# Decay factors of q applied in its turn, a completion signal moved to ScalarE, and one normalisation step issued one product later

## The chip, the cores and the metric

The kernel runs on one core of a Trainium2 chip. The metric is the device time of one execution in microseconds (us), the median of several executions. All runs of this study are recorded as fast (mean granted clock 0.986 to 1.0), so fast runs are compared with fast runs. The engines are TensorE (PE, with its weight loads as PEld), VectorE (DVE), ScalarE (ACT), GpSimd (POOL) and SyncE (SP), which issues most transfers (812 of 846 in the built program of the kernel before).

## The reference

Retention attention over 8 batches, 8 heads, 576 positions and a head size of 64 is followed by a SwiGLU feed-forward layer on the 4608 rows that result (cut to what matters):

```python
def _attn_ref(q, k, v):
    scores = scale * np.matmul(q, k.transpose(0, 1, 3, 2))
    Dmat = np.where(rel >= 0, gamma[:, None, None] ** rel[None, :, :], 0.0)
    return np.matmul(scores * Dmat[None], v)

def _moe_ref(x, w_gate, w_val, w_out, rms_g):
    xn = x / np.sqrt(np.mean(x * x, axis=-1, keepdims=True) + 1e-06) * rms_g
    g = xn @ w_gate
    return (g / (1.0 + np.exp(-g)) * (xn @ w_val)) @ w_out
```

## The kernel before

Attention runs in 32 jobs (a batch and a pair of heads each), in chunks of 64 positions. Jobs 0 to 7 come first, in the first 60 us, while weights are loaded and rounded beside them. The other jobs are strewn between the matmuls of the feed-forward layer, which works in combinations of weight blocks and of x (Strassen-like products, named x, y, z and w).

A job has these bursts of 64x64 matmuls on PE: scores and states, then values (the part within a chunk) and carried (what earlier chunks bring), both into the PSUM tile `av`. Jobs 0 to 7 have a turn ahead, which transposes q and k:

```python
    def turn(j):
        ...
                for e in range(2):
                    nc.tensor.matmul(
                        ps[side(e), c::NFULL], lhsT=d["q"][:, e, c], rhs=ident,
                        start=True, stop=True,
                    )
            t = d[nm + "T"] = att.tile([P, S], F32, tag=nm + "T", name=f"{nm}T_{j}")
            nc.scalar.copy(out=t[:, : NFULL * P], in_=ps)
        ...

    def values(j):
        ...
        d["valued"] = nc.gpsimd.memset(tick, 0.0)      # waits for the last matmul of values
        follow(d["valued"], mm)                        # carried's first matmul waits for it

    def carried(j):
        ...                                            # matmuls into av, then x on VectorE:
                    nc.vector.tensor_tensor(
                        out=x[to, first - c0 // L :: 2],
                        in0=av[odd][at, i * L : (i + n) * L].rearrange("p (c k) -> p c k", k=L),
                        in1=g.to_broadcast([at.stop - at.start, n, L]), op=ALU.mult,
                    )
```

In the stage from 217 to 260 us the last product group of the first row block, job 8, the weight combining on GpSimd (`combine`) and the scaling of the next block's x (`norm_2`) meet:

```python
        combine(1)
        slot(8, rest=False)
        following(8)
        for i, _ in enumerate(rest):
            if i == 2:
                norm_2(2)
        combine(0)
        slot(9)
```

Of the kernel before, what the change touches and what calls it, by code (L numbers as in the profile page):

```python
# [10 lines left out]
F32 = mybir.dt.float32  # L11
U32 = mybir.dt.uint32
AF = mybir.ActivationFunctionType
ALU = mybir.AluOpType
P = 128
L = P // 2


def _gamma(H):
    return 1.0 - 2.0 ** (-5.0 - np.arange(H, dtype=np.float64))  # L20


def _decay_tables(H, D):



    pairs = _gamma(H).reshape(H // 2, 2).T
    rows = np.repeat(pairs, D, axis=0)
    pos = np.arange(L)
    p = np.concatenate([pos, pos])  # L30
    gq = rows[:, :, None] ** (pos + L) / np.sqrt(D)
    t = pairs.T[None] ** -p[:, None, None], rows**L, gq, np.roll(gq, D, axis=0)
    return [np.ascontiguousarray(x).astype(np.float32) for x in t]


def _causal_table():

    return np.ascontiguousarray(np.tile(np.triu(np.ones((L, L), np.float32)), (2, 1)))
# [3 lines left out]
def kernel(  # L42
# [11 lines left out]
    nc = tc.nc  # L54
    B, H, S, D = q.shape
    NTOK, DM = out.shape
    DFF = moe_w_gate.shape[1]
    NHP = H // 2
    NF = DFF // P
    NC = S // L  # L60
    NFULL = S // P
    TAIL = S - NFULL * P
# [12 lines left out]
    const = ctx.enter_context(tc.tile_pool(name="const", bufs=1))  # L75
# [23 lines left out]
    ident = const.tile([P, P], F32, name="ident")  # L99
    mean_w = cell("mean_w", 1.0 / DM)  # L100
    mhalf = cell("mhalf", -0.5)
# [3 lines left out]
    causal = const.tile([P, L], F32, name="causal")  # L105
    gq = const.tile([P, NHP, L], F32, name="gq")
    gx = const.tile([P, NHP, L], F32, name="gx")
    gv = const.tile([P, NHP, 2], F32, name="gv")
    gc = const.tile([P, NHP], F32, name="gc")
    tick = const.tile([1, 1], F32, name="tick")  # L110
    rms_g = const.tile([P, NHP], F32, name="rms_g")
    w_out = const.tile([P, NF, DM], F32, name="w_out")
# [12 lines left out]
    w_up = [const.tile([P, 7 * 2, NH * P], F32, name=n) for n in ("w_gate", "w_val")]  # L125

    jobs = [(b, hp) for b in range(B) for hp in range(NHP)]
# [40 lines left out]
    def find_places():  # L168

        n = NFULL * 2 * D  # L170
        kv = {
            nm: [raw.tile([P, n], F32, tag=nm, name=f"first_{nm}_{i}", bufs=bufs) for i in range(bufs)]
            for nm, bufs in (("k", 4), ("v", 3))
        }
        other = raw.tile([P, S], F32, tag="qraw", name="first_k_7")[:, :n]
        sums = [ffn.tile([P, 3 * 2 * HU], F32, tag=t, name=f"first_{t}") for t in ("sums", "t1")]
        room = h_of[0].rearrange("p f t -> p (f t)")[:, 2 * NHP * 4 * P :]
        more = w_up[1][:, 8:].rearrange("p b f -> p (b f)")[:, 6 * DM :]
        return {
            "k": kv["k"] + kv["v"] + [other],  # L180
            "v": [t[:, i * n : i * n + n] for t in sums for i in range(2)]
            + [more[:, i * n : i * n + n] for i in range(3)] + [room],
        }
# [16 lines left out]
    def load_kv(j):  # L200
# [12 lines left out]
            out=t, in_=v[b, 2 * hp : 2 * hp + 2, NFULL * P :].rearrange("e p d -> p e d")  # L213
        )

    def turn(j):

        d = st[j]
        last = bank(f"turn_{j}_t")
        for nm in "qk":  # L220
            ps = bank(f"turn_{j}_{nm}")
            for c in range(NFULL):
                if nm == "k":
                    nc.tensor.transpose(
                        out=ps[:, c * P : c * P + P],
                        in_=d["k"][:, c].rearrange("p e d -> p (e d)"), identity=ident,
                    )
                    continue
                for e in range(2):
                    nc.tensor.matmul(  # L230
                        ps[side(e), c::NFULL], lhsT=d["q"][:, e, c], rhs=ident,
                        start=True, stop=True,
                    )
            t = d[nm + "T"] = att.tile([P, S], F32, tag=nm + "T", name=f"{nm}T_{j}")
            nc.scalar.copy(out=t[:, : NFULL * P], in_=ps)
        for i, nm in enumerate("qk"):
            o = slice(i * TAIL, i * TAIL + TAIL)
            nc.tensor.transpose(
                out=last[:, o], in_=d[nm + "t"].rearrange("p e d -> p (e d)"),
                identity=ident[:TAIL, :TAIL],  # L240
            )
        for i, nm in enumerate("qk"):
            o = slice(i * TAIL, i * TAIL + TAIL)
            nc.scalar.copy(out=d[nm + "T"][:, NFULL * P :], in_=last[:, o])
# [22 lines left out]
    def side(i):  # L267
        return slice(i * L, i * L + L)
# [75 lines left out]
    def values(j):  # L344

        d = st[j]
        av = d["av"] = [bank(f"av_{j}_{i}") for i in range(2)]
        for c in range(NC):
            i, odd = divmod(c, 2)
            for e in range(2):  # L350
                mm = nc.tensor.matmul(  # L351
                    av[odd][column(j, odd, e), i * L : i * L + L],
                    lhsT=d["v"][side(odd), i, e] if c < NC - 1 else d["vt"][:, e],
                    rhs=d["ret"][side(odd), e, i],
                    start=(c < 2), stop=False, skip_group_check=True,
                )


        d["valued"] = nc.gpsimd.memset(tick, 0.0)
        follow(d["valued"], mm)  # L360

    def carried(j):

        d = st[j]
        b, hp = jobs[j]
        av = d["av"]
        for c in range(1, NC):
            i, odd = divmod(c, 2)
            for e in range(2):
                mm = nc.tensor.matmul(  # L370
                    av[odd][column(j, odd, e), i * L : i * L + L], lhsT=d["sum"][side(e), c - 1],
                    rhs=d["qT"][side(e), c * L : c * L + L],
                    start=False, stop=(c >= NC - 2), skip_group_check=True,
                )
                if c == 1 and e == 0:
                    follow(mm, d["valued"])
        for c0, c1 in ((0, 2 * HU), (2 * HU, S)) if b % 2 == 0 else ((0, HU), (HU, S)):
            u, o = divmod(b * S + c0, U)
            if u not in x_of:
                x_of[u] = xp.tile([P, NHP, U], F32, tag="x", name=f"x_{u}")  # L380
            x = x_of[u][:, hp, o : o + c1 - c0].rearrange("p (c k) -> p c k", k=L)
            for first in (c0 // L, c0 // L + 1):
                i, odd = divmod(first, 2)
                n = -(-(c1 // L - first) // 2)
                moves = [(slice(0, P),) * 2]
                if column(j, odd, 0) != side(0):
                    moves = [(side(e), column(j, odd, e)) for e in range(2)]
                for to, at in moves:
                    g = (gq if to == at else gx)[at, hp].unsqueeze(1)
                    nc.vector.tensor_tensor(  # L390
                        out=x[to, first - c0 // L :: 2],
                        in0=av[odd][at, i * L : (i + n) * L].rearrange("p (c k) -> p c k", k=L),
                        in1=g.to_broadcast([at.stop - at.start, n, L]), op=ALU.mult,
                    )
        st[j] = {}
# [307 lines left out]
    for g in range(NG):  # L703
        for m, src in enumerate((moe_w_gate, moe_w_val)):
            for half in range(2):
                n = (half * NH + 2 * g) * P
# [31 lines left out]
    def load_chunks(n, queue=nc.scalar):  # L738

        nonlocal n_loads  # L740
        while n_loads < min(n, len(chunks)) and waits_at.get(spare(n_loads)) is None:
            load_chunk(n_loads, queue)
            n_loads += 1
# [102 lines left out]
    def start():  # L846

        h_of[0] = ffn.tile([P, NF, U], F32, tag="h", name="h_0")
        tables = list(zip((causal, gv, gc, gq, gx), (_causal_table(), *_decay_tables(H, D))))

        def table(i, queue):
            t, values_ = tables[i]
            src = nc.inline_tensor(values_, name=t.tensor.name + "_table")
            queue.dma_start(out=t, in_=src.ap())
# [5 lines left out]
        for _ in range(6):  # L860
            nc.tensor.matmul(warm[:, :P], lhsT=ones, rhs=ones, start=True, stop=True)
        first_places.update(find_places())
        load_chunks(1)
        for i in (1, 0, 2):
            table(i, nc.scalar)
        weights(3)
        for j in range(2 * NHP):
            load_first(j, {0: range(2), 1: range(2, H), NHP: range(H)}.get(j))
            if j == 1:
                table(3, nc.sync)  # L870
            load_chunks((1, 1, 1, 1, 2, 2, 2, 3)[j], nc.sync)
        table(4, nc.sync)
        nc.sync.dma_start(out=rms_g, in_=moe_rms_g.rearrange("(c p) -> p c", p=P))
        load_chunks(4, nc.sync)
# [4 lines left out]
        for j in range(2 * NHP):  # L879
# [7 lines left out]
            if j:  # L887
                u, c = divmod(j - 1, NHP)
# [54 lines left out]
        slot(8, rest=False)  # L943
        following(8)
        for i, _ in enumerate(rest):
            if i == 2:
                norm_2(2)
        combine(0)
        slot(9)
# [72 lines left out]
```

## Time and profile before

| | before |
|---|---|
| median time | 1151.92 us (1151.08 to 1154.7, 3 runs; with the fourth, of the result below, 1152.18) |
| span of the profiled run | 1151.4 us |
| PE busy | 1126.5 us, 98% |
| largest PE waits | issue 5.6 us in the first 60 us, tick 3.15 us, k of job 0 2.4 us |

The prediction below shows the lines for these. One line that it doesn't show turns out to matter, the line of the DMA queue that carries instructions (packets, MB, share of the engines' time):

```profile
q8 instruction: 83, 1.36, 0.5%
```

83 packets of 1.36 MB make 16.4 KB each. PE has 10524 multiplications and as many weight loads in the trace, and 167 waits and branches in the built program, 21,215 instructions in all: 21,215 / 83 = 255.6 instructions a packet. From these two counts I estimate that the queue carries PE's instruction stream in blocks of 256; the times of its packets, further below, agree.

### The profile page before, as it was taken

The page shows a single profiled execution, that of the slowest core. Times are in us where ns is not written, and L with a number is a line of the kernel's source. Part 1 is how long each engine was busy: PE and PEld are TensorE (multiplying, and loading weights), DVE is VectorE, ACT ScalarE, POOL GpSimd, SP SyncE. Part 2 cuts the span into 40 slices and gives each one's busy share as a digit, 9 for nine tenths or more (in the row PEclk, how much of TensorE's full clock was granted, in tenths as well). Part 3 has the DMA queues.
Part 4 walks back from the last instruction along what each step waited for, and adds up shares of the span by engine and source line. Part 5 has one row for each costly group of instructions (what it writes and reads, how often), then busy time and mean ns, then how long its engine had stood idle before and what let it go on. Part 6 is the DMA issues. An engine that isn't in the chain of part 4 may idle for free.

```text
span 1151.4 us, 24802 instructions
## 1 busy us (share of the span) xinstructions
PE 1126.5 (98%) x10524; PEld 1053.4 (91%) x10524; DVE 716.0 (62%) x1420; ACT 244.0 (21%) x480; POOL 50.8 (4%) x74
## 2 busy tenths in 40 slices
PE   8799999989999999999999999999999999999998
PEld 6655557989999999999999999999999999999998
DVE  5788858675675675365766675465576566445352
ACT  5546542002201211211221120120220220120210
POOL 0000000570000000000000000000000000000000
PEclk8999999999999999999999999999999999999999
DMA  8764336335453565044345456306436503403304
GB/s 203 207 184 147 109 131 193 56 59 117 115 130 67 146 141 160 1 105 102 97 119 73 116 144 119 114 29 120 117 80 140 144 19 93 128 1 99 122 1 110
DMA packets 292943, 125.42 MB, mean 109 GB/s; under 512 B 270432, under 2 KB 275808, under 8 KB 292832
## 3 DMA queue, kind: packets, MB, share of 16 engines
q1 hardware_dynamic: 282688, 107.66, 38.1%
q10 hardware_dynamic: 10144, 16.16, 4.3%
q8 instruction: 83, 1.36, 0.5%
q14 instruction: 28, 0.23, 0.1%
HBM read 108.83 MB, written 14.94 MB: 108 GB/s over the span
## 4 chain that ended last, share of the span: by engine, by line
PE 90%; DVE 3%; DMA 2%; POOL 1%; ACT 1%; issue 1%; SPq 0%; DVEq 0%; POOLq 0%; ACTq 0%
PE x L507 14%; PE w L507 14%; PE z L507 13%; PE up L564 8%; PE xo L629 8%; PE wo L629 7%; PE zo L629 7%; PE y L507 7%; PE yo L629 4%; PE av L351 2%; PE av L370 2%; PE s L280 2%; POOL w_gate L811 1%; PE s L300 1%; DMA w_gate<-in_moe_w_out_dram 1%
## 5 line engine op out<-in xcount | busy, mean ns | idle before, releaser
L531 ACT COPY m<-x 128x384 f32<-128x384 f32 x60 | 28.8, 479 | 449.8 <-PE x L507 425.5
L629 PE MATMUL xo<-h,w_out 128*128 128x192 f32 x528 | 90.3, 328 | 0.0
L507 PE MATMUL w<-sums,w_val 128*128 128x192 f32 x480 | 88.6, 328 | 0.6 <-DVE c L514 0.3
L507 PE MATMUL x<-x,w_gate 128*128 128x192 f32 x480 | 89.0, 329 | 0.0
L507 PE MATMUL x<-x,w_val 128*128 128x192 f32 x480 | 88.8, 328 | 0.0
L507 PE MATMUL z<-x,w_gate 128*128 128x192 f32 x480 | 87.8, 326 | 0.0
L507 PE MATMUL w<-sums,w_gate 128*128 128x192 f32 x480 | 87.8, 326 | 0.0
L507 PE MATMUL z<-x,w_val 128*128 128x192 f32 x480 | 87.8, 326 | 0.0
L629 PEld LDWEIGHTS xo<-h,w_out 128*128 128x128 f32 x528 | 85.9, 190 | 0.6
L629 PE MATMUL wo<-h,w_out 128*128 128x192 f32 x504 | 85.3, 326 | 0.0
L629 PEld LDWEIGHTS wo<-h,w_out 128*128 128x128 f32 x504 | 82.5, 190 | 0.0
L514 DVE TENSOR_TENSOR u<-m,y 128x384 f32<-128x384 f32 x60 | 33.1, 552 | 79.2 <-PE y L507 79.1
L507 PEld LDWEIGHTS w<-sums,w_val 128*128 128x128 f32 x480 | 79.2, 190 | 2.9 <-DVE c L514 2.9
L507 PEld LDWEIGHTS x<-x,w_gate 128*128 128x128 f32 x480 | 79.6, 191 | 0.5
L507 PEld LDWEIGHTS z<-x,w_gate 128*128 128x128 f32 x480 | 79.8, 190 | 0.0
L507 PEld LDWEIGHTS x<-x,w_val 128*128 128x128 f32 x480 | 79.1, 190 | 0.6
L507 PEld LDWEIGHTS z<-x,w_val 128*128 128x128 f32 x480 | 79.6, 190 | 0.0
L507 PEld LDWEIGHTS w<-sums,w_gate 128*128 128x128 f32 x480 | 79.6, 190 | 0.0
L514 DVE TENSOR_TENSOR h<-u,w 128x384 f32<-128x384 f32 x60 | 33.0, 551 | 71.0 <-PE w L507 71.0
L526 ACT ACTIVATE h<-h 128x384 f32<-128x384 f32 x90 | 47.1, 523 | 88.6 <-DVE h L514 88.6
L564 PE MATMUL up<-x,w_gate 128*128 128x384 f32 x192 | 63.3, 488 | 0.9 <-DVE x L476 0.7
L564 PE MATMUL up<-x,w_val 128*128 128x384 f32 x192 | 62.7, 487 | 0.2 <-ACT w_val L572 0.2
(170 smaller groups left out, 1769.8 us busy)
## 6 DMA issues: line engine op xcount, KB each, us to landing
w_out<-w_blocks SPq DMA_DIRECT2D x70, 768.0 KB, 5.1
out_dram<-o SPq DMA_DIRECT2D x368, 24.0 KB, 1.6
qraw<-in_q_dram SPq DMA_DIRECT2D x96, 72.0 KB, 2.7
kraw<-in_k_dram SPq DMA_DIRECT2D x96, 72.0 KB, 2.8
k<-in_k_dram SPq DMA_DIRECT2D x48, 128.0 KB, 3.0
v<-in_v_dram SPq DMA_DIRECT2D x48, 128.0 KB, 2.9
w_out<-in_moe_w_gate_dram ACTq DMA_DIRECT2D x5, 1024.0 KB, 5.8
w_out<-in_moe_w_out_dram ACTq DMA_DIRECT2D x3, 1024.0 KB, 4.9
```

Source lines behind the costliest of these rows:

```text
L280: nc.tensor.matmul(s[side(odd), e, i * L : i * L + L], lhsT=d["kT"][side(e), c * L : c * L + L], rhs=d["qT"][side(e), c * L : c * L + L], ...
L300: nc.tensor.matmul(o[side(e)], lhsT=d["k"][side(odd), i, e], rhs=d["v"][side(odd), i, e], start=True, stop=True,)
L351: mm = nc.tensor.matmul(av[odd][column(j, odd, e), i * L : i * L + L], lhsT=d["v"][side(odd), i, e] if c < NC - 1 else d["vt"][:, e], rhs= ...
L370: mm = nc.tensor.matmul(av[odd][column(j, odd, e), i * L : i * L + L], lhsT=d["sum"][side(e), c - 1], rhs=d["qT"][side(e), c * L : c * L + L],
L507: nc.tensor.matmul(ps[:, i * HU : i * HU + HU], lhsT=w_up[m][:, 2 * blk + c, cut], rhs=t_of[u][blk][:, c], start=(start and i == c == 0), ...
L514: nc.vector.tensor_tensor(out=o, in0=a, in1=pairs_of(ps), op=ALU.add)
L526: nc.scalar.activation(out=o, in_=c, func=AF.Silu)
L531: nc.scalar.copy(out=s1, in_=pairs_of(x_))
L564: nc.tensor.matmul(ps[:, :U], lhsT=w_up[m][:, 4 * half + c, i * P : i * P + P], rhs=x_of[u][:, c], start=(c == 0), stop=(c == NHP - 1),)
L629: nc.tensor.matmul(ps[:, i * HU : i * HU + HU], lhsT=a[:, c, i * P : i * P + P], rhs=rhs[:, c], start=(start and i == c == 0), stop=False, ...
L811: nc.gpsimd.tensor_tensor(out=o, in0=a, in1=b, op=op)
```

## The change

Its intent was threefold: to take the multiplication of x by q's decay off VectorE in the eight first jobs, by putting the factors into the matmul that turns q; to free job 8's carried from GpSimd's queue; and to scale x of block 2 one product later, so that zo no longer waits behind it. Core of the diff, with cuts marked:

```diff
+    def make_factors(j):
+        for e in range(2):
+            main, tail = factors(j, e)
+            g = turned[:, 2 * jobs[j][1] + e]
+            if j < 2:
+                for i in range(NFULL):
+                    nc.scalar.activation(
+                        out=main[:, i], in_=ident, func=AF.Copy, scale=g[:, i : i + 1]
+                    )
 ... (one more for the tail; GpSimd tensor_tensor for j >= 2)
-                        ps[side(e), c::NFULL], lhsT=d["q"][:, e, c], rhs=ident,
+                        ps[side(e), c::NFULL], lhsT=d["q"][:, e, c], rhs=factors(j, e)[0][:, c],
 ... (the tail of q: two 64x64 matmuls in place of one transpose)
-        d["valued"] = nc.gpsimd.memset(tick, 0.0)
+        if j == 2 * NHP:
+            d["valued"] = nc.scalar.copy(out=tick, in_=mhalf[:1])
+        else:
+            d["valued"] = nc.gpsimd.memset(tick, 0.0)
 ... (x of jobs 0 to 7: nc.scalar.copy in place of nc.vector.tensor_tensor)
+        for i in (5, 1, 0, 2):
+            table(i, nc.scalar)
         load_chunks(1)
-        for i in (1, 0, 2):
-            table(i, nc.scalar)
+        for j in range(NHP):
+            make_factors(j)
 ...
-            if i == 2:
+            if i == 3:
                 norm_2(2)
```

More of the change, by code (lines that the diff above doesn't have):

```diff
@@ L32, in _decay_tables @@
     t = pairs.T[None] ** -p[:, None, None], rows**L, gq, np.roll(gq, D, axis=0)
+    at = np.stack([(4 * np.arange(P) + i) % L for i in range(4)] + [np.arange(P) % L], axis=1)
+    t += (_gamma(H)[None, :, None] ** (at[:, None, :] + L) / np.sqrt(D),)
     return [np.ascontiguousarray(x).astype(np.float32) for x in t]
@@ L109 @@
     gc = const.tile([P, NHP], F32, name="gc")
+    turned = const.tile([P, H, NFULL + 1], F32, name="turned")
     tick = const.tile([1, 1], F32, name="tick")
@@ L214, in load_kv, with factors @@
         )
+    def factors(j, e):
+        h = 2 * jobs[j][1] + e
+        main = w_up[0][:, h, 2 * P : 6 * P].rearrange("p (i t) -> p i t", t=P)
+        return main, w_up[1][:TAIL, h, 4 * P : 4 * P + TAIL]
+    def make_factors(j):
[7 more added lines that the diff above has]
+                    )
+                nc.scalar.activation(
+                    out=tail, in_=ident[:TAIL, :TAIL], func=AF.Copy, scale=g[:TAIL, NFULL:]
+                )
+                continue
+            nc.gpsimd.tensor_tensor(
+                out=main, in0=ident.unsqueeze(1).to_broadcast([P, NFULL, P]),
+                in1=g[:, :NFULL].unsqueeze(2).to_broadcast([P, NFULL, P]), op=ALU.mult,
+            )
+            nc.gpsimd.tensor_tensor(
+                out=tail, in0=ident[:TAIL, :TAIL],
+                in1=g[:TAIL, NFULL:].to_broadcast([TAIL, TAIL]), op=ALU.mult,
+            )
     def turn(j):
@@ L235, in turn @@
             nc.scalar.copy(out=t[:, : NFULL * P], in_=ps)
-        for i, nm in enumerate("qk"):
-            o = slice(i * TAIL, i * TAIL + TAIL)
-            nc.tensor.transpose(
-                out=last[:, o], in_=d[nm + "t"].rearrange("p e d -> p (e d)"),
-                identity=ident[:TAIL, :TAIL],
-            )
+        for e in range(2):
+            nc.tensor.matmul(
+                last[side(e), :TAIL], lhsT=d["qt"][:, e], rhs=factors(j, e)[1],
+                start=True, stop=True,
+            )
+        nc.tensor.transpose(
+            out=last[:, TAIL : 2 * TAIL], in_=d["kt"].rearrange("p e d -> p (e d)"),
+            identity=ident[:TAIL, :TAIL],
+        )
         for i, nm in enumerate("qk"):
@@ L388, in carried @@
                 for to, at in moves:
+                    if j < 2 * NHP:
+                        nc.scalar.copy(
+                            out=x[to, first - c0 // L :: 2],
+                            in_=av[odd][at, i * L : (i + n) * L].rearrange("p (c k) -> p c k", k=L),
+                        )
+                        continue
                     g = (gq if to == at else gx)[at, hp].unsqueeze(1)
@@ L848, in start @@
         h_of[0] = ffn.tile([P, NF, U], F32, tag="h", name="h_0")
-        tables = list(zip((causal, gv, gc, gq, gx), (_causal_table(), *_decay_tables(H, D))))
+        tables = list(zip((causal, gv, gc, gq, gx, turned), (_causal_table(), *_decay_tables(H, D))))
         def table(i, queue):
@@ L868, in start @@
             load_first(j, {0: range(2), 1: range(2, H), NHP: range(H)}.get(j))
-            if j == 1:
-                table(3, nc.sync)
             load_chunks((1, 1, 1, 1, 2, 2, 2, 3)[j], nc.sync)
+        table(3, nc.sync)
         table(4, nc.sync)
```

## The prediction

> **What bounds the kernel now.** The engine table of the page comes first, because it says which engine can matter at all.
>
> ```profile
> PE 1126.5 (98%) x10524; PEld 1053.4 (91%) x10524; DVE 716.0 (62%) x1420; ACT 244.0 (21%) x480; POOL 50.8 (4%) x74
> ```
>
> TensorE (PE) is busy for 98% of 1151.4 us, so only its 25 us of idle time, its matmul count and its clock can change the end. VectorE (DVE), ScalarE (ACT) and GpSimd (POOL) count only where PE waits for them. Next, the table of PE's waits, summed by releaser (total, count, longest):
>
> ```profile
> PE av L370 <- issue: 4.1, 3, 2.3
> PE av L370 <- POOL tick L359: 3.7, 3, 3.1
> PE turn_k L224 <- DMA first_k<-in_k_dram: 2.4, 1, 2.4
> PE s L280 <- issue: 1.4, 2, 1.0
> ...
> PE av L351 <- ACT kT L235: 1.1, 4, 0.3
> PE zo L629 <- DVE u4o L638: 0.8, 1, 0.8
> PE s L280 <- ACT kT L235: 0.8, 1, 0.8
> ```
>
> The largest removable wait is one of 3.1 us on the tick. It sits in the stage at 217 to 260 us, read from the timeline of all engines (start, duration, line, what, and in brackets the idle time before):
>
> ```profile
> 235.03 17.56 POOL L811 TENSOR_TENSOR w_gate<-w_gate 128x512 f32<-128x512 f32 x12
> ...
> 237.07 1.50 DVE L487 TENSOR_TENSOR sums<-x,sums 128x384 f32<-128x384 f32 x1
> ...
> 241.22 2.28 DVE L641 TENSOR_TENSOR h<-h 128x1152 f32<-128x1152 f32 x1
> ...
> 243.69 4.06 PE L629 MATMUL wo<-h,w_out 128*128 128x192 f32 x24
> ...
> 252.53 0.09 POOL L359 MEMSET tick<- 1x1 f32 x1
> 252.67 0.69 PE L370 MATMUL av<-qT,sum 64*64 64x64 f32 x32 [3.15 <-POOL tick L359]
> ```
>
> The tick is a 0.09 us memset queued behind 17.56 us of GpSimd's weight combining. The stretch-by-stretch view shows what the wait costs afterwards:
>
> ```profile
> 253.00:254.00 1.00, 1.00 (x31) 0.93 (x21) 0.55 (x2) 0.00 (x0) 0.00 (x0) 1.00 0.39 64
> 254.00:255.00 1.00, 1.00 (x6) 1.00 (x5) 0.94 (x4) 0.00 (x0) 0.00 (x0) 0.61 0.30 46
> 255.00:256.00 1.00, 1.00 (x5) 1.00 (x4) 0.88 (x5) 0.48 (x1) 0.00 (x0) 0.50 0.06 5
> ```
>
> The third column from the end is the granted clock. It is 0.50 from about 254.4 to 257.7, and eight matmuls that take 1.30 us elsewhere take 2.0 and then 2.48: some 1.9 us lost. The tick thus costs 3.15 + 1.9 = 5.0 us. The start is the other stage, on ScalarE's timeline:
>
> ```profile
> 7.90 0.33 ACTq L854 DMA_DIRECT2D causal<-causal_table  x1
> 8.28 0.44 ACTq L854 DMA_DIRECT2D gc<-gc_table  x1
> 8.76 0.59 ACT L235 COPY qT<-turn_q 128x512 f32<-128x512 f32 x1 [6.54 <-DMA gv<-gv_table]
> 9.24 0.59 ACT L235 COPY kT<-turn_k 128x512 f32<-128x512 f32 x1
> ```
>
> Job 0's scores start at 9.89, right after these copies. ScalarE is busy without a gap until 17.37; from there PE sets the pace, about 5.9 us a job.
>
> [...] L487 takes 1.50 us under the combining and .557 elsewhere, L641 2.28 against 1.33, while L638, with one input in PSUM, keeps .55. [...] The "issue" waits of PE (0.35, 1.07, 2.33, 1.01 and 0.81 in the first 60 us, 5.6 in all) lie at regular distances in the instruction stream[...].
>
> **The change, part by part.**
>
> *Factors in the turn.* q's decay now comes from the right-hand side of the matmul that turns q, a diagonal of factors instead of the identity. The 16 matmuls a job stay; the tail has one more 64x64 matmul, about .05 us, 8 x .05 = +0.4. The diagonals of the first two head pairs are 16 ACTIVATEs of 128x128 and 4 of 64x64, and they stand in ScalarE's queue before the first qT copy. From rows with a scale operand (128x256 at a pitch of .41, 64x64 at .24) I interpolate .295 for 128x128: 16 x .295 + 4 x .24 = 5.7 us. They follow, in the same queue, the issue of the first weight chunk, which waits for the second half of k_0. That landed at 7.9 in the kernel before, in competition with the chunk; with the chunk held back I estimate 5.0 to 5.5 (393 GB/s moved at 4 to 6 us). So qT is copied at 5.5 + 5.7 = 11.2 instead of 8.76: +2.4. The whole ScalarE-bound start shifts by it. GpSimd's diagonals (pairs 2 and 3) take about 4 x 1.6 us, from 19.29/12 for a 128x512 operation, and are ready by 15, well before job 2.
>
> *x by ScalarE, other buffer waits.* For jobs 0 to 7 four VectorE multiplications (.94 us a job) become four ScalarE copies. VectorE is full only at 50 to 67 us, where values(7) waited 0.55 and the first up products 0.71; I give back 0.3 of these. The order of the instructions moves too: PSUM banks of the turn rotate differently, so that in slots 2 to 7 the turn's tail no longer waits for the qT copy (0.15 a slot) nor the values for the kT copy (0.24): 6 x 0.39 = -2.3. The states will instead sometimes wait for v's scaling on ScalarE, at an estimate of +0.1 a slot, +0.6. Net of this part with the added matmuls: -2.3 + 0.6 + 0.4 - 0.3 = -1.6.
>
> *Tick by ScalarE.* Job 8's tick now follows its values at once: -5.0 with the clock loss, and it is all on PE's path.
>
> *x of the second half scaled one product later.* PE no longer waits 0.8 for u4o. But the scaling and sums now stand on VectorE behind u2o, u4o, c and T, which come at the end of yo, 234.2. Chain: these four 2.3, scaling 4 x .55 = 2.2, sums .61 + 3 x 1.51 = 5.1 (GpSimd combines until 252.5), T .58, h of L641 2.3, together 12.5, so h is ready at 246.7 and wo starts about 246.9 to 247.8, against 243.69. PE runs dry at 242.6: an idle of 4.3 to 5.2 us and[...] a half clock afterwards worth 1.5 to 1.9. From wo on: 4.0, values and scores 1.8, carried .7, x and y 2.6, clock 1.5: y ends at about 258.0, where it ended at 257.84. So the tick's gain is given back: net of these two parts 0 (+-1.5).
>
> Sum: 1151.9 + 2.4 - 1.6 + 0 = 1152.7.
>
> **The rivals.**
> 1. The tick's 5 us come through. [...] It would make 1152.7 - 5 = 1147.7, with the start as estimated.
> 2. The start is not the bound. The loads of q, k and v run until 52 us, and ScalarE waited for v of job 5 at 36 to 38, so a late start may be taken up by later waits: -2.4, or 1150.3. Against it: PE had hardly a DMA wait after 8.02.
> 3. Bad luck in the instruction fetch. 52 more ScalarE instructions, 32 fewer VectorE ones and other loads shift where PE's blocks fall against full DMA queues: the 5.6 us may become 3 or 9, with a clock loss of up to 2 behind any longer one: 1150 to 1157.
> 4. ScalarE's start costs more: the chunk's issue at 6.5 rather than 5.5, and chunk 0's rounding, now later, delays qT_1. +2, or 1154.7.
>
> **Range and chances.** The central value is the sum, drawn 0.4 towards rivals 1 and 2, which both lie lower: 1152.3. Errors are about 2 for the start, 1.5 for the 217 to 260 stage, 2.5 for fetch and clock, 1 for the slots; in quadrature 3.6, and 1.28 x 3.6 = 4.6, so 1147.7 to 1156.9. Two per cent is 23 us, more than all terms together, so "within 2%" is nearly certain.
>
> **What would show it.** Right: the first qT copy at about 11.2 behind 20 ACTIVATEs; no tick wait at carried(8); wo waiting 4 us for DVE's L641 with L487 still near 1.5 us; y of job 8 ending some 1 to 3 us later than 257.84 by the clock of the span only because of the start. Wrong: a wo that follows zo at once (rival 1), a PE that stands at the same time at 62 us as before despite the late start (rival 2), or "issue" waits whose sum differs from 5.6 by more than 3 (rival 3).

## The result

The changed kernel is correct and slower: 1164.17 us median (1161.17 to 1165.04, 4 runs) against 1152.18. The ratio is 1.0096, with a 95% interval of 1.0071 to 1.0121. Ratios here are the mean time of one kernel's fast runs over the mean of the other's fast runs of the same rounds, so not quite the ratio of the medians quoted. That is "within 2%", but it lies well outside the predicted range of 1147.7 to 1156.9.

The engine line of the page:

```profile
PE 1133.6 (98%) x10548; PEld 1060.5 (91%) x10548; DVE 709.1 (61%) x1388; ACT 255.3 (22%) x533; POOL 56.0 (5%) x81
```

VectorE has 32 instructions less and ScalarE 53 more, as planned. PE has 24 more multiplications and 24 more weight loads, 48 instructions, because 16 float32 matmuls, with two records each in the trace, take the place of 8 transposes with one record each. By the built programs there are also 12 more waits (179 against 167). Keep the sum, 60, in mind. PE's waits in the changed kernel (total, count, longest):

```profile
PE av L409 <- issue: 7.3, 4, 3.0
PE wo L674 <- DVE h L686: 4.7, 1, 4.7
PE turn_q L263 <- ACT w_gate L233: 3.1, 2, 2.4
...
PE s L316 <- ACT kT L268: 1.2, 1, 1.2
PE x L552 <- issue: 1.1, 1, 1.1
...
PE z L552 <- DVE u L559: 0.6, 1, 0.6
```

The tick's 3.1 is gone, the wait of wo for h is there, and "issue" in carried (L409) has grown. Where the time came from is read by the start of the same PE instruction in both traces:

| PE instruction | before | after | offset |
|---|---|---|---|
| scores of job 0 | 9.89 | 12.78 | +2.89 |
| mean square of block 0, second half | 67.45 | 69.85 | +2.40 |
| mean square of block 2 | 204.79 | 207.35 | +2.56 |
| z of job 8's slot | 257.68 | 262.05 | +4.37 |
| a mean square | 329.97 | 333.95 | +3.98 |
| another | 600.79 | 604.10 | +3.31 |
| another | 694.73 | 700.69 | +5.96 |
| another | 870.93 | 880.51 | +9.58 |
| another | 963.98 | 974.52 | +10.54 |

So 2.6 us come in the start and 1.8 in the stage around 240 us (2.7 by values of job 9, 273.38 before and 278.62 after). Until 600 us 1.9 are won back, most of them where a stall of the kernel before, in job 10, is gone. Then 7.2 come between 600 and 970 us, where the change has no line at all.

**The late part.** PE's timeline there, one line for each of the four stalls, with what runs ahead of it (start, duration, line, what, count of records, idle time before):

```profile
652.79 0.56 PE L409 MATMUL av<-qT,sum 64*64 64x64 f32 x23
654.73 0.34 PE L409 MATMUL av<-qT,sum 64*64 64x64 f32 x8 [1.37 <-issue]
...
676.97 0.34 PE L409 MATMUL av<-qT,sum 64*64 64x64 f32 x5 [1.24 <-issue]
...
846.11 0.35 PE L409 MATMUL av<-qT,sum 64*64 64x64 f32 x9 [1.71 <-issue]
...
931.99 0.65 PE L552 MATMUL x<-x,w_val 128*128 128x192 f32 x3 [1.10 <-issue]
```

Each stall falls inside the burst of carried or just behind it, after 24, 27 and 23 of its 32 records, and at the last after all 32 and five more; in no case does the profile show PE waiting for another engine. The stretches around the third (the last three columns are granted clock, DMA share and GB/s):

```profile
842.00:843.00 1.00, 1.00 (x52) 0.80 (x54) 0.81 (x3) 0.00 (x0) 0.00 (x0) 1.00 1.03 432
843.00:844.00 1.00, 1.00 (x82) 1.00 (x76) 0.45 (x1) 0.00 (x0) 0.09 (x1) 1.00 0.50 182
...
846.00:847.00 1.00, 0.90 (x11) 0.83 (x11) 0.47 (x2) 0.00 (x0) 0.00 (x0) 0.80 0.00 0
847.00:848.00 1.00, 1.00 (x5) 1.00 (x5) 0.94 (x4) 0.00 (x0) 0.00 (x0) 0.50 0.00 0
```

The DMA engines are full of a weight load until 843.5, at the time when PE races through some 80 records a microsecond; then PE stands, and afterwards it runs at half clock. That one stall cost 3.6 us of offset: 1.71 of waiting, 1.9 of slow matmuls.

**The place in the stream.** If I number PE's instructions in the built programs (two for each record, one for each wait), I can say at which number modulo 256 each stall in carried begins:

| kernel, job | first instruction of carried | records done | place |
|---|---|---|---|
| before, 3 (35.5 us) | 182 | 6 | 194 |
| before, 6 (57.6 us) | 157 | 18 | 193 |
| before, 10 (295.6 us) | 139 | 27 | 193 |
| after, 2 (30.6 us) | 139 | 27 | 193 |
| after, 21 (652.8 us) | 145 | 24 | 193 |
| after, 22 (675.0 us) | 139 | 27 | 193 |
| after, 26 (843.8 us) | 147 | 23 | 193 |
| after, 29 (929.2 us) | 119 | 32 + 5 | 193 |

All lie at the boundary of one block of 256. Jobs whose boundary lies there but with a DMA share of 0.45 or less ahead of the burst (20, 27 and 28 in the changed kernel; 9 and 11 before) have no stall. Neither have jobs 11 to 14, 17 to 19 and 25 of the changed kernel, whose boundary comes earlier, after 0 to 20 records, although a load ran into the bursts of 14 and 18 (DMA share 0.90 from 402 to 403 us and 0.71 from 570 to 571 us). From here the theory: where PE runs through a whole block of short instructions in 1.9 to 2.8 us (the four stalled jobs of the next table) while a weight load fills the queues, the next block is late. The 60 added instructions moved the places of all later bursts.

The packed trace also holds the start and end of each of the 83 packets of the instruction queue, which no view prints. For six jobs of the changed kernel:

| job | previous boundary, passed at | packet | boundary in or behind carried | PE goes on at |
|---|---|---|---|---|
| 21 | 651.44 | 652.55 to 653.50 | 653.35 | 654.73 |
| 22 | 673.75 | 674.57 to 675.48 | 675.73 | 676.97 |
| 26 | 842.48 | 843.72 to 844.71 | 844.40 | 846.11 |
| 29 | 928.07 | 929.62 to 930.61 | 930.89 | 931.99 |
| 20 | 630.47 | 629.40 to 630.79 | 632.34 | no stall |
| 27 | 866.80 | 865.96 to 866.90 | 868.71 | no stall |

Beside a load the packet starts some 2 us later in relation to the block, and PE goes on 1.2 to 1.5 us after it has landed. The same holds for all issue waits of the two kernels: their traces have twelve ahead of PE's multiplications. All twelve, the seven of the first 60 us included, lie at places 193 and 194, and each ends 1.22 to 1.71 us after a packet of this queue has landed. In the last two whole microseconds before the ends of the five early ones of the kernel before (22.72, 31.69, 38.19, 50.66 and 59.23) the DMA share was between 0.65 and 1.15; in the microsecond of the first, which was the shortest, it was 0.11.

**The stage around 240 us.** Timeline of the changed kernel:

```profile
237.37 4.06 PE L674 MATMUL xo<-h,w_out 128*128 128x192 f32 x24
241.27 4.06 PE L674 MATMUL zo<-h,w_out 128*128 128x192 f32 x24
...
246.15 1.50 DVE L532 TENSOR_TENSOR sums<-x,sums 128x384 f32<-128x384 f32 x1
...
248.07 1.91 DVE L686 TENSOR_TENSOR h<-h 128x1152 f32<-128x1152 f32 x1
...
250.04 7.13 PE L674 MATMUL wo<-h,w_out 128*128 128x192 f32 x24 [4.71 <-DVE h L686]
```

wo waits 4.71 for VectorE's h, which stands behind the scaling and the sums (1.50 to 1.58 each beside GpSimd's combining; the median of the kernel's sums is 0.56), and then takes 7.13 instead of 4.06. The granted clock (third column from the end) was 0.50 for most of it:

```profile
249.00:250.00 1.00, 0.00 (x0) 0.00 (x0) 1.00 (x2) 0.00 (x0) 1.00 (x1) 0.64 0.35 52
...
255.00:256.00 1.00, 1.00 (x5) 1.00 (x5) 0.00 (x0) 0.00 (x0) 0.15 (x1) 0.50 0.35 51
256.00:257.00 1.00, 1.00 (x7) 0.88 (x5) 0.00 (x0) 0.00 (x0) 0.00 (x0) 0.95 0.17 25
```

**The start.** ScalarE's timeline:

```profile
5.51 0.42 ACTq L781 DMA_DIRECT2D w_out<-in_moe_w_gate_dram  x1
6.04 1.28 ACT L233 ACTIVATE w_gate<-ident,turned 128x128 f32<-128x128 f32 x4 [3.82 <-DMA gc<-gc_table]
...
11.68 0.56 ACT L268 COPY qT<-turn_q 128x512 f32<-128x512 f32 x1
...
14.12 1.15 ACT L813 ACTIVATE w_gate<-w_gate,least 128x1024 f32<-128x1024 uint32 x1
...
17.54 0.56 ACT L268 COPY qT<-turn_q 128x512 f32<-128x512 f32 x1
```

The first weight chunk is issued at 5.51 (0.93 before), the diagonals fill 6.04 to 11.68, and the second qT copy comes at 17.54 (14.63 before).

### The profile page after: what moved, and what is told of

It reads as the page before. It is cut to its first block, busy times and chain, and to the rows that moved or that the text cites. A ratio compares the mean times of both kernels' runs of the same rounds, so it can differ in the third digit from the quotient of the medians.

```text
span 1161.8 us, 24888 instructions
## 1 busy us (share of the span) xinstructions
PE 1133.6 (98%) x10548; PEld 1060.5 (91%) x10548; DVE 709.1 (61%) x1388; ACT 255.3 (22%) x533; POOL 56.0 (5%) x81
## 3 DMA queue, kind: packets, MB, share of 16 engines
q8 instruction: 83, 1.36, 0.5%
## 4 chain that ended last, share of the span: by engine, by line
PE 90%; DVE 4%; ACT 3%; DMA 2%; issue 1%; DVEq 0%; POOL 0%; POOLq 0%
PE x L552 13%; PE w L552 13%; PE z L552 13%; PE wo L674 8%; PE xo L674 8%; PE zo L674 8%; PE up L609 8%; PE y L552 7%; PE yo L674 4%; PE av L387 2%; PE av L409 1%; PE s L316 1%; PE s L336 1%; DMA w_gate<-in_moe_w_out_dram 1%; ACT w_gate L813 1%
## 5 line engine op out<-in xcount | busy, mean ns | idle before, releaser
L674 PE MATMUL wo<-h,w_out 128*128 128x192 f32 x504 | 88.4, 334 | 4.7 <-DVE h L686 4.7
L674 PEld LDWEIGHTS wo<-h,w_out 128*128 128x128 f32 x504 | 85.4, 196 | 5.0 <-DVE h L686 5.0
```

The source lines that it names most:

```text
L674: nc.tensor.matmul(ps[:, i * HU : i * HU + HU], lhsT=a[:, c, i * P : i * P + P], rhs=rhs[:, c], start=(start and i == c == 0), stop=False, ...
```

## The experiments

Fourteen kernels ran, all with correct results, five rounds each. "The kernel before" had medians of 1152.27 to 1152.59 in these rounds.

| run | median us | ratio to before (95%) |
|---|---|---|
| a_pad14 | 1156.72 | 1.0044 (1.0029 to 1.0058) |
| b_pad15 | 1161.63 | 1.0078 (1.0065 to 1.0091) |
| b_tick | 1150.82 | 0.9991 (0.9980 to 1.0003) |
| a_two | 1155.96 | 1.0035 (1.0023 to 1.0047) |
| b_tick_p28 | 1155.14 | 1.0023 (1.0010 to 1.0036) |
| a_two_p14 | 1152.55 | 1.0001 (0.9984 to 1.0019) |
| a_two_g1_p14 | 1151.24 | 0.9989 (0.9967 to 1.0011) |
| a_fetch | 1163.72 | 1.0093 (1.0076 to 1.0110) |
| a_gall | 1163.45 | 1.0086 (1.0073 to 1.0099) |
| a_gall_c | 1161.31 | 1.0079 (1.0061 to 1.0097) |
| best1 | 1154.40 | 1.0012 (0.9997 to 1.0026) |
| best2 | 1155.60 | 1.0019 (1.0005 to 1.0034) |
| best3 | 1149.53 | 0.9976 (0.9958 to 0.9993) |
| best4 | 1147.16 | 0.9955 (0.9937 to 0.9973) |

### Moving PE's places: a_pad14 and b_pad15

```diff
         for _ in range(6):
             nc.tensor.matmul(warm[:, :P], lhsT=ones, rhs=ones, start=True, stop=True)
+        for _ in range(14):                      # 15 on the kernel before
+            nc.tensor.matmul(
+                warm[:64, :64], lhsT=ones[:64, :64], rhs=ones[:64, :64], start=True, stop=True
+            )
```

> The changed kernel with 14 small matmuls (64x64 by 64x64) behind the warm-up, in a time in which PE waits anyway: they shift every later PE instruction by 56 places. All five stalls of PE put down to issue in the two traces that lie in carried lie at the same place modulo 256 of PE's instruction stream (193 in my count of the built programs). Theory (a boundary of the fetched 256-instruction blocks falls in the dense 64x64 matmuls of carried while a weight load fills the DMA queues): with this shift no loaded job from job 8 on has a boundary there, so the four stalls at 654, 677, 846 and 932 us (5.4 us, and 1.2 of clock loss) are gone, offset to the kernel before constant from 330 us on within 0.5 us, time about 6.5 us less than the changed kernel, 1157 to 1158. Stalls of the first 60 us may move by 2 to 3 us either way. Rival (the late 6.6 us are an aftereffect of the late start or of buffers and loads moved by the change): the time stays at 1164 within 1.5 us, and the stalls stay in jobs 21, 22, 26 and 29.

Measured: 1156.72, 7.5 us less than the changed kernel, though 14 matmuls were added. No issue wait is left behind 75 us, the wait of wo (4.69) is unchanged, and the offset to the kernel before goes from 4.1 us at 330 us to 3.6 at the end. The rival falls. One job shows that a boundary and a load aren't enough: in job 29 the boundary comes after 9 records of carried with the DMA share at 0.94 to 1.01 from 921 to 924 us, and nothing stalls. PE had passed the boundary before 3.7 us earlier, where in the four late stalls of the changed kernel it was 1.9 to 2.8.

> The kernel before with 15 of the same small matmuls: every later PE instruction is 60 places on, which puts it from job 8 on at the places that it has in the changed kernel. Fetch theory: the stall of job 10 (0.92) goes, and stalls of 1.1 to 1.7 us appear in carried of jobs 21, 22 and 26 and just behind that of job 29, as in the changed kernel: 5.4 - 0.9 + 1.2 of clock = +5.7 us, so 1157 to 1158, give or take 2 to 3 of other stalls in the first 60 us. Rival: same time as before, 1152 within 1 us.

Measured: 1161.63, 9.4 us more than the kernel before, with nothing else changed; that is more than expected. The four stalls of the changed kernel appear in the kernel before, in the same jobs after the same counts of records:

```profile
655.51 0.34 PE L370 MATMUL av<-qT,sum 64*64 64x64 f32 x8 [1.67 <-issue]
...
678.04 0.34 PE L370 MATMUL av<-qT,sum 64*64 64x64 f32 x5 [1.54 <-issue]
...
847.15 0.35 PE L370 MATMUL av<-qT,sum 64*64 64x64 f32 x9 [1.58 <-issue]
...
931.65 0.65 PE L507 MATMUL x<-x,w_val 128*128 128x192 f32 x3 [1.39 <-issue]
```

They sum to 6.2 us, and from 600 to 964 us the offset to the kernel before grows by 6.4; the stall of job 10 is gone, as expected. The rest came in the first 75 us, where the issue waits rose from 5.6 to 8.1.

### The tick alone: b_tick

```diff
-        d["valued"] = nc.gpsimd.memset(tick, 0.0)
+        if j == 2 * NHP:
+            d["valued"] = nc.scalar.copy(out=tick, in_=mhalf[:1])
+        else:
+            d["valued"] = nc.gpsimd.memset(tick, 0.0)
```

> The kernel before with job 8's tick made by ScalarE and nothing else. My prediction's account of the tick: carried of job 8 follows at once, wait of 3.15 and clock loss of 1.9 gone, y of job 8 ends 5.0 us earlier, 1147. Rival 1 (the wait moves elsewhere, to the stage after, for example x of job 8 waiting for GpSimd's combined weights or job 9 for VectorE): 1150 to 1152. PE's places shift by 2 only, so the late fetch stalls stay as before.

Measured: 1150.82, only 1.4 us less, with an interval that takes in 1. The tick's gain is there at first: values of job 9 begin at 268.42 against 273.38, 4.96 earlier, of which 0.76 stem from before 230 us. So 4.2 are the tick's: 5.0 less a new wait of z for VectorE's u (0.63) and small terms. Then it is lost:

```profile
273.15 0.42 PE L373 MATMUL av<-qT,sum 64*64 64x64 f32 x9 [2.53 <-issue]
```

Job 9 has its boundary after 22 to 24 records in both kernels. In the kernel before the DMA share was 0.00 to 0.07 ahead of its carried, the last line below. Here, because PE is some 5 us earlier, a weight load is under way:

```profile
269.00:270.00 1.00, 1.00 (x83) 1.00 (x77) 0.65 (x2) 0.00 (x0) 0.09 (x1) 1.00 1.04 418
270.00:271.00 1.00, 0.62 (x41) 0.48 (x33) 0.68 (x2) 0.00 (x0) 0.00 (x0) 1.00 0.98 393
```

```profile
274.00:275.00 1.00, 1.00 (x81) 1.00 (x76) 0.59 (x2) 0.00 (x0) 0.09 (x1) 1.00 0.00 0
```

By 329 us the lead of 4.96 has shrunk to 1.1. The time lies in rival 1's range and not at the theory's 1147, but neither named this cause. Job 10 adds a detail: its boundary comes after 26 records, and its load ended at about 293.6, some 1.5 us ahead of carried. Its burst took 1.11 us instead of 0.68, where in the kernel before, with the load lasting until 295.4, it stalled by 0.92.

### x of block 2 scaled where it was: a_two

```diff
-            if i == 3:
+            if i == 2:
                 norm_2(2)
```

> The changed kernel with the scaling of x of the second half put back by one product (as in the kernel before); tick by ScalarE and the rest stay, PE's places are the same. Theory: the wait of wo for h (4.71) and the half clock behind it (wo 7.13 instead of 4.06, so 3.07) go, zo's wait of 0.8 for u4o and tick-free carried come: y of job 8 ends 4.71 + 3.07 - 0.8 = 7 us earlier than in the changed kernel, 1157; the four late stalls stay. Rival (VectorE's chain under GpSimd's combining is as long either way, so a wait of a similar size comes in another place): 1162 to 1164.

Measured: 1155.96, 8.2 us less than the changed kernel; expected were 7. wo follows zo at once and takes 4.06; zo waits 0.75 for u4o again; the four late stalls stay, between 0.97 and 1.67. In this stage, from 204 us to values of job 9, the offset to the kernel before grows by 2.7 in the changed kernel and falls by 4.2 here. So the third part of the change, meant to save 0.8, cost about 7 us. The two traces are 7.7 us apart; 2.0 less in the late part and 1.3 more in the start, both at the same places, make up the rest.

This run also has a stall without a load, with the DMA share at 0.00 to 0.08 from 52 to 57 us, in carried of job 5:

```profile
56.64 0.27 PE L409 MATMUL av<-qT,sum 64*64 64x64 f32 x1 [1.15 <-issue]
```

The boundary ahead of it had stalled, too (0.35 at 52.91), and the packet started at 54.04, after that stall. So a load is one way to make a block late, not the only one.

### Is the gain of the tick kept with safe places? b_tick_p28 and a_two_p14

Edits: the tick of b_tick with 28 of the small matmuls behind the warm-up; a_two with 14 of them.

> The kernel before with the tick of job 8 by ScalarE and 28 small matmuls behind the warm-up, which put the boundaries of the fetched blocks outside of carried in every loaded job from job 8 on (job 9 included, which a weight load had reached in the run with the tick alone, and which stalled there by 2.53 us with a half clock of about 1.5 us behind it). Fetch theory: no issue stall above 0.5 us after 70 us; the tick's gain of 4.2 us at job 9's values is now kept to the end: 1146 to 1148, plus or minus 2 for the stalls of the first 60 us. Rival (the gain is lost in something else behind job 9): 1150 to 1152.

Measured: 1155.14. No issue wait is left behind 75 us, as expected, but the added matmuls took 0.11 us a record, where carried takes 0.022, and ran for 6.23 us; why they were so slow isn't shown. Scores of job 0 began at 13.68 instead of 9.89, and the time rose. The time says nothing of the tick, but the trace does: from scores of job 8 to those of job 10 the offset to the kernel before falls from 6.59 to 2.39, by the tick's 4.20. Nothing behind it takes this back, and at the end the offset is 0.71.

> The changed kernel with x of the second half scaled where the kernel before does it, and with the 14 small matmuls. If the two effects are separate they add: 1164.2 - 7.5 - 8.2 = 1148.5, and against the kernel before with tick and padding it is slower by the late start alone, 2.5 to 3.5 less 1.5 of buffer waits in the slots. If they overlap: 1153 to 1156.

Measured: 1152.55, where addition gave 1148.5. The late issue waits are 0.00 and wo doesn't wait, so both effects went as they should. But the profiled run had 6.6 us of issue waits in the first 75 us, against 3.4 in the changed kernel, and its offset at 204 us was 6.9 instead of 2.6. The padding had moved the early places, too. That is a part of the answer alone: a_pad14 and a_two had 5.8 and 6.5 of such waits themselves, and offsets of 3.5 and 3.8. Addition also counted twice the 2.0 us by which the late part was shorter in a_two.

### The start: a_two_g1_p14, a_gall, a_gall_c

```diff
-            if j < 2:                  # ScalarE makes the diagonals
+            if j < 1:                  # a_two_g1_p14; j < 0 in a_gall and a_gall_c
```

> The same with the diagonals of the second head pair made by GpSimd, too, so that ScalarE has 10 instead of 20 ACTIVATEs before the first qT copy. Theory (the start is bound by ScalarE's queue): the first qT copy at 8.9 instead of 11.7, job 0's scores at 10.1 instead of 12.7, and the 2.7 us are kept to the end: 2.7 us faster than the run with 20. Rival (turn of job 1 then waits for GpSimd, or the start is bound by the loads): 0 to 1 us faster.

Measured: 1151.24, 1.3 us less than a_two_p14, with intervals that overlap. Scores of job 0 began at 11.70, 1.0 earlier and not 2.6: with the chunk's issue still ahead, ScalarE began its ten diagonals at 6.15 and PE turned q only behind them.

> The changed kernel with all diagonals made by GpSimd and none by ScalarE; PE's places stay as they are. In the changed kernel GpSimd had begun at 4.2 us with 1.3 us a head, while ScalarE began at 6.0 because the issue of the weight chunk ahead in its queue waited for k. Theory (the late start is ScalarE's queue): job 0's first head is ready at 5.5, second at 6.8, q is turned by 8, job 0's scores start at 9 to 9.5 instead of 12.78, and the 3.3 to 3.8 us are kept: 1160.5, give or take 2 for the stalls of the first 60 us; the late stalls stay. Rival (the start is taken up by the loads later on): 1163 to 1164.

Measured: 1163.45, like the changed kernel within the intervals and in the range of the rival. Scores began at 9.24, as expected, but the gain didn't last. Two timelines of this run, PE's and ScalarE's, show why:

```profile
13.21 1.97 PE L263 MATMUL turn_q<-w_gate,h 128*64 128x128 f32 x16 [1.36 <-DMA h<-in_q_dram]
```

```profile
13.58 1.15 ACT L813 ACTIVATE w_gate<-w_gate,least 128x1024 f32<-128x1024 uint32 x1 [2.67 <-DVE w_gate L797]
...
17.00 0.56 ACT L268 COPY qT<-turn_q 128x512 f32<-128x512 f32 x1
```

q of job 1 lands late beside the late chunk (PE waits 1.36 for it, until 13.21), and the chunk's rounding stands ahead of job 1's qT copy. Carried of job 0 began at 21.17, against 20.31 in the changed kernel and 17.61 before.

```diff
         table(5, nc.scalar)
         load_chunks(1)                 # a_gall_c: ahead of the other tables again
         for i in (1, 0, 2):
             table(i, nc.scalar)
```

> The changed kernel with all diagonals by GpSimd (as the run before) and with the first weight chunk issued right behind the table of factors, not behind the landing of k. In the run with the diagonals alone job 0 began at 9.24 us, but q of job 1 landed only at 13.2, behind the late chunk, and qT of job 1 was copied at 17.00 (14.63 in the kernel before, 17.54 in the changed one) behind the chunk's rounding. Theory (two things made the start late, ScalarE's diagonals and the chunk's late issue, and either alone suffices): qT of job 1 is now copied by 15, carried of job 0 starts at 17.5 to 18.5 instead of 20.3, and 2 to 3 us are kept up to 67 us, apart from the fetch stalls; late stalls stay: 1161, give or take 2. Rival (the loads of q, k, v bound the first slots anyway): carried of job 0 at 20 or later.

Measured: qT of job 1 is copied at 15.39 and carried of job 0 begins at 19.56, 0.75 earlier than in the changed kernel but still 2 us later than before. The time, 1161.31, has an interval that overlaps with that of the changed kernel. So half of the theory holds: the chunk's late issue is a part of it. What holds the other 2 us isn't shown. Job 1's scores waited 1.08 for ScalarE's scaled v in this run; that is one candidate.

### A load moved away: a_fetch

```diff
-                if i in (1, 3):
-                    fetch()
-                    fetch()
 ...
                 behind(u, i)
+                if i in (1, 3):
+                    fetch()
+                    fetch()
```

> The changed kernel with the loads of combined weights issued behind the attention slot of the same step instead of ahead of it; PE's places are the same. Theory (a stall needs both a boundary in carried and a weight load at that time): the stall of job 26, whose step issued the load just ahead of it, goes with the half clock behind it, 2.9 us; those of jobs 21, 22 and 29 stay, as the loads ahead of them come in another order anyway: 1161.3. If the boundary alone made the stalls: all four stay, 1164.

Measured: 1163.72; the expectation was missed, because the edit didn't do what I wanted. A load was still issued at 837.4 us and filled the queues ahead of job 26 (share 0.96 from 841 to 843), which stalled by 1.30. But a load now ran ahead of job 27, too (share 0.98 and 0.90; it was 0.00 to 0.06 in the changed kernel). Job 27 has the same place in both programs, had no stall in the changed kernel, and has one here:

```profile
867.43 0.34 PE L409 MATMUL av<-qT,sum 64*64 64x64 f32 x5 [0.82 <-issue]
```

With job 9 in b_tick that is the second case in which the place stayed, a load came, and a stall came with it.

### All mended: best1 to best4

best1: the changed kernel with all diagonals by GpSimd, `norm_2` at 2, and 14 repeated matmuls at the head of job 0's values. best2: the kernel before with the tick by ScalarE and 28 repeated matmuls there. best3: a_gall_c with `norm_2` at 2, and best4: the kernel before with the tick, both with the repeated matmuls in job 8 instead:

```diff
-        for c in range(NC):
+        for c in [0] * (14 if j == 8 else 0) + list(range(NC)):   # best4; 7 in best3; j == 0 in best1, best2
```

> All three mended: the changed kernel with all diagonals by GpSimd, x of the second half scaled where the kernel before does it, and 14 matmuls repeated at the head of job 0's values (their results are overwritten), where PE waits for ScalarE, so that no boundary of a block lies in carried of a loaded job from job 8 on. Sum: 1152.5 of the run with two of these and the padding at the very start, less 3.5 for the start: 1149, give or take 2. Against the kernel before that is faster by some 3 us.

Measured: 1154.40, not 1149.

> The kernel before with job 8's tick by ScalarE, and 28 repeated matmuls at the head of job 0's values instead of behind the warm-up, where they had cost 3.8 us of start. No late stall is left, the tick's 4.2 us and job 10's stall of 0.9 are gained, the repeated matmuls cost at most 1.2: 1148, give or take 2 for the stalls of the first 60 us.

Measured: 1155.60, not 1148. In both, no late issue wait is left, and the stalls of the first 75 us are 5.8 and 9.5 us. For best2 that is more than in any kernel with the early places of the kernel before (5.58 there, 3.82 in b_tick, 2.84 in best4), so the repeated matmuls in job 0 had moved the early places to worse ones. For best1 this isn't shown: kernels with the early places of the changed one had 3.4 to 6.5.

> The same with x of the second half scaled as in the kernel before and 14 repeated matmuls at the head of job 8's values, so that no late boundary falls in carried of a loaded job while the places of the first eight jobs stay those of the changed kernel. Sum from the kernel before: tick -4.2, job 10's stall -0.9, repeated matmuls +0.6, extra matmuls and waits in the slots -1.5, start 0: 1146.5; with the stalls of the first 60 us, which other runs had between 3.4 and 9.5, give or take 3.

Measured: 1149.53, 3 us more than expected, at the edge of the range given. It beats the kernel before by 0.24%, with an interval that leaves out 1.

> The kernel before with the tick by ScalarE and 28 repeated matmuls at the head of job 8's values: the first eight jobs are as in the kernel before in every place, and the late boundaries are out of carried of loaded jobs. Tick -4.2, job 10's stall -0.9, repeated matmuls +1.2: 1148.3, give or take 1. If stalls at block boundaries are not what took the tick's gain in the run with the tick alone: 1151.

Measured: 1147.16 (1145.87 to 1148.77), 0.45% less than the kernel before and 1.5% less than the changed one. It is the fastest of all. In its profiled run values of job 9 began 5.15 us earlier than in the kernel before: 2.58 of that lay already at 204 us, where issue waits were 2.84 instead of 5.57, and the tick brought 4.2 less 1.6 for the repeated matmuls. The 2.58 aren't the edit's by anything shown, as every place up to there is that of the kernel before. The comparison of best2 and best4 is the plainest: the same instructions in the same numbers, 28 matmuls of them at another place, 8.4 us apart by the medians (of two rounds) and 7.1 in the profiled runs, where 6.6 are early issue waits (9.48 against 2.84).

## Why the prediction was wrong

**The sum left out the late fetch stalls; that step failed.** Rival 3 named the mechanism, from the issue waits of the kernel before, but the text treated it as luck of the first 60 us, worth nothing on average, and added zero for the rest of the program. The 60 added instructions moved the boundaries into or just behind carried of four jobs with a weight load: 5.4 us of waits and about 1.9 of clock behind one of them, 7.2 us of offset where the sum had 0. b_pad15 and a_pad14 show it from both sides. The places could have been counted before the run, as both programs were there, and the kernel before had such a late stall: the line "PE av L370 <- issue: 4.1, 3" that the prediction shows holds 0.92 us at 297.26, outside of the first 60 us. The early part of rival 3 went the other way: 3.4 us instead of 5.6. In all the issue waits grew from 6.5 to 8.9 us; against the 5.6 that the prediction names, 8.9 is over 3 more, its own sign of rival 3.

**The stage at 217 to 260 us: right mechanism, one term mis-sized.** The chain of VectorE, the idle of 4.3 to 5.2 us (4.71) and L532 near 1.5 us came as worked out. The half clock was put at 1.5 to 1.9 us, the loss read off the kernel before, where the granted clock was 0.50 from 254.2 to 257.6, for 3.4 us. Here it was 0.50 from 249.3 to 256.1, for 6.8 us, and cost 3.07 on wo alone. The chain's first sum took 1.58 instead of the 0.61 read off the kernel before. The stage gave +1.8 at z of job 8 and +2.7 by values of job 9, where z had waited 0.63 for VectorE's u, instead of 0. a_two shows the part's cost. That GpSimd's combining makes the sums slow was read from durations alone (1.5 beside it, 0.56 at 346 us without) and is not shown: no run took the combining away, and the 0.61 of the kernel before, at 233.33, lay beside it, too.

**The tick: right, with its gain exposed to the first step's error.** Predicted -5.0, measured -4.2 at job 9's values; in b_tick a stall took it, in b_tick_p28 and best4 it stayed. The clock's share was read a little too high: by the starts of x, y and z (253.30, 255.16, 257.68) the two products lost 1.8 and not 1.9.

**The start: size nearly right, cause half right.** +2.4 predicted, +2.89 measured at job 0's scores; the first qT copy came at 11.68 instead of 11.2. The reason given, 20 ACTIVATEs in ScalarE's queue, isn't the only one: without them (a_gall) the start stays late, because the late chunk delays q of job 1 and the qT copy. That was rival 4's second half.

**The slots: not confirmed.** -1.6 was predicted for slots 2 to 7. Between carried of jobs 0 and 4 the offset fell from 2.70 to 1.48, with waits for issue 0.8 shorter and more half clock (6.8 us from 34.2, where the kernel before had 3.4 from 39.2). By 67 us it stood at 2.40 again, 0.3 below the start, although the issue waits up to there were 2.1 shorter. At 49.49 the tail of job 6's turn waited 0.55 for ScalarE's copies of x, a wait that I had not listed. The parts of this are not told apart by a run.

**Rival 2** (loads take up the late start) has b_tick_p28 against it: job 0 began 3.8 us late, and at 217 us the offset was 6.6, with issue waits 0.4 longer than in the kernel before. **Rival 1** fell, as predicted.

**Open:** the size of the early stalls. In the traces of the two kernels all lie at block boundaries, but the sum was between 2.84 and 9.48 us over the runs, and with the same early places it still differed by up to 3 us (3.44 in the changed kernel, 6.46 in a_two). The remaining 2 us at the start of a_gall_c are open as well.

## What to carry to other kernels

Here 60 instructions added to PE's stream, at the start, moved all later block boundaries, and stalls of 1.4 to 1.7 us came in or behind four bursts of short matmuls beside full DMA queues, some 640 us and more behind the edit; in b_pad15 that and the early stalls were 0.8% of the time, with nothing else changed. So before a difference of this size is credited to an edit, look at the issue waits in both traces, and compare at two or three shifts of the stream. The removed wait on the tick was worth its 4.2 us where nothing behind it took them back (b_tick_p28, best4); in b_tick the earlier PE met a load at a boundary and lost 2.53 at once. Look as well at what is put ahead of a weight load in its queue: in the changed kernel the first chunk, behind four tables, was issued at 5.51 us instead of 0.93.

## What the traces show of late blocks and of half clock

- Of the some 83 block boundaries of the changed kernel six had an issue wait. At a boundary in or just behind carried beside a weight load, a wait behind 75 us took 0.7 us (a_gall_c) to 2.5 us (b_tick), 5.4 us in the sum of the late part in the changed kernel and 6.2 in b_pad15; in the first 60 us one took 4.0 us (states, best2).
- The four late ones of the changed kernel came where PE had passed the boundary before only 1.9 to 2.8 us earlier and a load lasted into the job's bursts; the packet then started 0.8 to 1.6 us after that boundary. With a load that ended 1.5 us ahead of carried 0.4 us were lost (job 10 of b_tick). With a load and 3.7 us between the boundaries (job 29 of a_pad14) there was no stall, and in the start one of 1.15 us came without a load (job 5 of a_two). What decides is not shown beyond these cases.
- In the changed kernel the granted clock was 0.50 for 3.4 us from 846.6, just behind 1.71 us of idle PE (844.4 to 846.1), and for 6.8 us from 249.3, with 4.71 us of idle PE ahead of wo. Behind the waits of 1.37, 1.24 and 1.10 us at the three other late stalls it stayed 1.00.
